# The front of a fused attention and gMLP kernel: load order, tile 0 and 1's epsilon, and the turns of tiles 1 to 3

## The chip, the cores and the metric

The kernel runs on one core of one Trainium2 chip. A time is the device time of one execution in microseconds; the time of a kernel is the median of its runs. Engines are named as in the profile: PE (TensorE, matmuls), PEld (TensorE's weight loads), DVE (VectorE), ACT (ScalarE), POOL (GpSimd), SP (SyncE, which here only issues loads and stores).

## The reference

```python
def reference(A_x, A_wqkv, A_wo, B_x, B_w_in, B_w_sp, B_b_sp, B_w_out):
    x = A_x                                   # (1, 2048, 512) bf16
    xn = layernorm(x)                         # eps 1e-5, no scale
    return x + A(xn, A_wqkv, A_wo) + B(xn, B_w_in, B_w_sp, B_b_sp, B_w_out)

def A(x, wqkv, wo):    # 32 heads of 16; each position looks at 8 positions back, 2 apart
    q, k, v = split(x @ wqkv)
    logits = q . k[pos - 2 * w] / 4           # w = 0..7, masked before the start
    return (softmax(logits) . v[pos - 2 * w]) @ wo

def B(x, w_in, w_sp, b_sp, w_out):            # w_in: 512 x 1376, so two halves of 688
    z = gelu(x @ w_in)
    z1, z2 = z[..., :688], layernorm(z[..., 688:])
    g = w_sp @ z2 + b_sp                      # mixes the 2048 positions
    return (z1 * g) @ w_out
```

## The kernel before

The 2048 tokens are 16 tiles of 128 tokens. The front of the kernel brings each tile from its load to the first matmul, in these steps (i is the tile):

- `x{i}`: the load of the tokens, 128 x 512, issued by SP (`load_x`). `wz0` and `wz1` load the z2 half of `w_in` (512 rows as four blocks of 128, "kc", two blocks in each load); they are issued by ACT. A memset on VectorE into `w_z[1]` stands ahead of them: the first load waits for it.
- `b{i}`, `ag{i}`: VectorE's statistics (`bn_stats`) and their aggregate to mean and variance (`bn_aggr`).
- `gr{i}`: GpSimd adds epsilon (L179) and raises to the power -1/2 (L180).
- `n{i}`: VectorE normalises the tile (L183); for tile 0 in two halves, `n0a` and `n0` (L187).
- `T{i}`: TensorE turns the tile in four 128x128 transposes (L216) into a bank of PSUM (`aux`, two in turn); `Tc{i}`: ACT copies it to `xnT` (L219). Tile 0 is turned in two halves, `T0a` and `T0`. From tile 8 on the turn is a transposing DMA (`t{i}`).
- `z{i}`: eight matmuls on TensorE (L234), four kc by two halves of 344 columns, into one of three PSUM buffers `mm`; `h{i}`: ACT's gelu of it (L251). For tile 0, `z0a` is the four matmuls of kc 0 and 1, and `z0b` those of kc 2 and 3.

Ahead of the first turn TensorE runs ten matmuls on constants (`wu`, L463), and after `T0` the turn of the bias (`B`, L470, whose 4 KB load `b16` GpSimd issues) and three short spins (`wd`, L463).

Every engine runs its steps strictly in the order of a list written out by hand (`pe`, `act`, `dve`, `pool`, `sp`); a step also waits for the steps it names. No scheduler moves anything. Behind the front come the z1 half, the projections to q, k and v, the attention products, the mixing with `w_sp` and the two output projections, all in the same lists; they are not touched.

Of the kernel before, what the change touches and what calls it, by code (L numbers as in the profile page):

```python
# [26 lines left out]
FH = 688  # L27
F = 2 * FH
# [4 lines left out]
EPS = 1e-5  # L33
# [9 lines left out]
def kernel(  # L43
# [48 lines left out]
    w_z = [wts[:, C * (3 * D + n * FH):C * (3 * D + (n + 1) * FH)].rearrange("p (k f) -> p k f", k=C) for n in (1, 0)]  # L92
# [17 lines left out]
    z2 = z2_r[:].rearrange("p (i f) -> p i f", i=NT)  # L110
# [4 lines left out]
    xs = z1_r[:, 0:NT * D].rearrange("p (i d) -> p i d", i=NT)  # L115
# [14 lines left out]
    mm = [ps.tile([P, 2, D], F32, name=f"mm{n}") for n in range(3)]  # L130
# [39 lines left out]
    LX = [0, 1, 2, 3, 4, 5, 6, 6] + [8] * 4 + [12] * 4  # L170

    def bn(i):
        V.bn_stats(stats[:, i, :], xs[:, i, :])  # L173

    def ag(i):
        V.bn_aggr(mv[:, i, :], stats[:, i, :])

    def root(i, n):
        G.tensor_scalar(rstd[:, i:i + n], mv[:, i:i + n, 1], EPS, 1.0, ALU.add, ALU.mult)  # L179
        G.tensor_tensor(rstd[:, i:i + n], rstd[:, i:i + n], mhalf[:, 0:n], ALU.pow)  # L180

    def norm(eng, i):
        eng.tensor_scalar(xn[i % 8], xs[:, i, :], mv[:, i, 0:1], rstd[:, i:i + 1], ALU.subtract, ALU.mult)  # L183

    def norm_half(n):
        c = slice(n * D // 2, (n + 1) * D // 2)
        V.tensor_scalar(xn[0][:, c], xs[:, 0, c], mv[:, 0, 0:1], rstd[:, 0:1], ALU.subtract, ALU.mult)  # L187

    for i in range(NT):
        op_(f"b{i}", [f"x{LX[i]}"], lambda i=i: bn(i))  # L190
        op_(f"ag{i}", [f"b{i}"], lambda i=i: ag(i))
        op_(f"gr{i}", [f"ag{i}"], lambda i=i: root(i, 1))
        if i == 0:
            op_("n0a", ["gr0"], lambda: norm_half(0))
            op_("n0", ["n0a"], lambda: norm_half(1))
        else:
            op_(f"n{i}", [f"gr{i}"] + ([tok(i - 8)] if i >= 8 else []), lambda i=i: norm(V, i))
        if i >= NPE:
            op_(f"t{i}", [f"n{i}"], lambda i=i: SP.dma_start_transpose(xnT[:, :, i * P:(i + 1) * P], xn[i % 8]))
# [21 lines left out]
    def make_T0():  # L221
        t0 = psum("aux", "T0a", "Tc0a", ["n0a"], lambda t: turn(0, t, (0, 1)))
        t1 = psum("aux", "T0", "Tc0", ["T0a", "n0"], lambda t: turn(0, t, (2, 3)))
        op_("Tc0a", ["T0a"], lambda: turned(0, t0, 0, 2))
        op_("Tc0", ["T0"], lambda: turned(0, t1, 2, 4))

    def make_T(i):
        t = psum("aux", f"T{i}", f"Tc{i}", [f"n{i}"], lambda t: turn(i, t))
        op_(f"Tc{i}", [f"T{i}"], lambda: turned(i, t))


    def z_half(t, i, part, hh, kcs=range(C)):
        for kc in kcs:
            PE.matmul(t[:, hh, 0:FHALF], xnT[:, kc, i * P:(i + 1) * P], w_z[part][:, kc, hh * FHALF:(hh + 1) * FHALF],  # L234
                      start=(kc == 0), stop=(kc == C - 1))
# [2 lines left out]
        for hh in range(2):  # L238
            z_half(t, i, part, hh)

    for n in range(2):
        op_(f"wz{n}", [], lambda n=n: A.dma_start(w_z[1][:, 2 * n:2 * n + 2, :], wi_d[:, 2 * n:2 * n + 2, FH:F]))
    op_("wk", [], lambda: SP.dma_start(w_k, wq_d[:, :, D:2 * D]))
    op_("wq", [], lambda: SP.dma_start(w_q, wq_d[:, :, 0:D]))
    op_("wv", [], lambda: SP.dma_start(w_v, wq_d[:, :, 2 * D:3 * D]))
# [9 lines left out]
    def make_z(i):  # L255
        t = psum("mm", f"z{i}", f"h{i}", [tok(i), "wz0", "wz1", "Bc"], lambda t: z_part(t, i, 1))
        op_(f"h{i}", [f"z{i}"], lambda: z2_gelu(i, t))

    def make_z0():
        t0 = psum("mm", "z0a", "h0", ["Tc0a", "wz0"], lambda t: [z_half(t, 0, 1, hh, (0, 1)) for hh in range(2)])  # L260
        op_("z0b", ["z0a", tok(0), "wz1"], lambda: [z_half(t0, 0, 1, hh, (2, 3)) for hh in range(2)])
        op_("h0", ["z0b"], lambda: z2_gelu(0, t0))

    def z2_bn(i):
        for hh in range(2):
            V.bn_stats(zst[:, i, hh, :], z2[:, i, hh * FHALF:(hh + 1) * FHALF])
        V.bn_aggr(zmv[:, i, :], zst[:, i].rearrange("p a b -> p (a b)"))
# [200 lines left out]
    def make_B():  # L468
        def turn_b(t):
            PE.transpose(t.bitcast(BF16)[:, 0:NT], b16[:], ident[0:NT, 0:NT])  # L470
# [118 lines left out]
    for n, (t, c) in enumerate(pieces):  # L589
# [1 line left out]
        op_(f"Sl{n}", [f"Fl{n}"], lambda n=n, c=c: (SP, A, SP)[n].dma_start(out2[il * P:(il + 1) * P, c], o_of(il)[:, c]))  # L591


    pe = """wu T0a T0 B wd z0a T1 z0b T2 z1 T3 z2 T4 z3 T5 z4 T6 z5 T7 z6 z7 y0 y1 z8 z9 z10 z11 z12 z13 z14
        k0 k1 q0 q1 k2 k3 q2 q3 k4 k5 q4 q5 k6 k7 q6 q7
        v0 v1 v2 v3 v4 v5 v6 v7 z15 y2 y3 y4 y5 y6 y7 y8 y9 y10 y11 y12 y13 y14 y15
        M0 M1 M2 M3 M4 M5 M6 M7 M8 M9 M10 M11 M12 M13 M14 M15
# [1 line left out]
    for n in pe:  # L599
        a, x = n[0], n[1:]  # L600
        if n in do:
            continue
        if n == "T0a":
            make_T0()
        elif a == "T":
            make_T(int(x))
        elif n == "z0a":
            make_z0()
        elif a == "z":
            make_z(int(x))  # L610
        elif a == "y":
            make_y(int(x))
        elif a in "qkv":
            make_heads(a, int(x))
        elif a == "M":
            make_M(int(x))
        elif a == "B":
            make_B()
    op_("GL", [], lambda: A.preload_act_table(ACT.Gelu_apprx_tanh))
    op_("EL", ["yg15"], lambda: A.preload_act_table_set("natural_log_exp_and_others"))  # L620

    act = """wz0 wz1 GL Tc0a Tc0 Bc Tc1 Tc2 h0 Tc3 h1 Tc4 h2 Tc5 h3 Tc6 h4 Tc7 h5 h6 h7 yg0 yg1 h8 h9 sq8 h10 h11 sq9 h12 h13 h14 sq10
        kc0 sq11 kc1 qc0 sq12 qc1 kc2 sq13 kc3 sq14 qc2 qc3 kc4 kc5 qc4 qc5 kc6 kc7 qc6 qc7
        vc0 vc1 zn8 vc2 zn9 vc3 zn10 vc4 zn11 vc5 vc6 vc7 h15 sq15
        yg2 yg3 yg4 yg5 yg6 yg7 yg8 yg9 zn12 yg10 zn13 yg11 zn14 yg12 zn15 yg13 yg14 yg15 EL
        e0 G0 i0 G1 e1 i1 G2 G3 G4 G5 G6 G7 G8 G9 G10 G11 G12 G13 G14 G15""".split()
    act += [f"E{i}" for n in (0, 1) for i in groups[n]]
    dve = """b0 ag0 b1 ag1 n0a n0 b2 ag2 n1 b3 n2 ag3 b4 ag4 n3 b5 ag5 n4 b6 ag6 b7 n5""".split()
    for i in range(6, NT):
        dve += [f"ag{i + 1}"] * (i + 1 < NT) + [f"b{i + 2}"] * (i + 2 < NT) + [f"n{i}"]  # L630
    dve += """zt0 zt1 zt2 zt3 zt4 zt5 zn0 zn1 zn2 zn3 zt6 zt7 zn4 zn5 zn6 zn7
# [62 lines left out]
```

## Time and profile before

| | |
|---|---|
| median of 3 runs | 200.33 us (200.26 to 200.45) |
| the profiled execution | 200.27 us, of which the profile's span is 198.5 us |
| PE busy | 194.2 us, 98% of the span |
| DVE busy | 178.4 us, 90% |
| ACT busy | 89.4 us, 45% |
| POOL busy | 49.3 us, 25% |
| granted TensorE clock over the span | 1.000 |

Times in the profile are counted from the start of the span. A row of the timeline has start, length, engine, line, operation and tiles, and in brackets how long the engine stood idle just before and what released it; equal operations that follow one another are merged with their count. Matmuls are pipelined: a merged row ends when its last result is out, and the next row can start before that. A load's line is that of the issue; the time to landing is from the issue to the moment its last engine reports.

### The profile page before, as it was taken

The numbers are of one execution on the slowest core, as the hardware profiler recorded it, in microseconds if no ns is written. First come the engines' busy times: TensorE is split into PE (matmuls) and PEld (weight loads), VectorE is DVE, ScalarE is ACT, GpSimd is POOL, SyncE is SP. The second block draws the span as 40 slices with busy tenths as digits, with TensorE's granted clock in tenths as the row PEclk, the third lists the DMA queues.
The fourth block names the chain that finished last, engine by engine and source line by source line (L and its number), as shares of the span: only waits on it lengthen the run. The fifth ranks groups of instructions, "written<-read, shape, count | busy, mean of one in ns | idle before, by whom it ended". The sixth has DMA issues, their size and how long they took to land.

```text
span 198.5 us, 4606 instructions
## 1 busy us (share of the span) xinstructions
PE 194.2 (98%) x1957; PEld 122.0 (61%) x1960; DVE 178.4 (90%) x205; ACT 89.4 (45%) x130; POOL 49.3 (25%) x83
## 2 busy tenths in 40 slices
PE   8999999999999999999999999999999999999993
PEld 2566666666666666666666666666666654444442
DVE  4899896999979999988999999999999999997244
ACT  2587797875559885991462311111222110044000
POOL 5567222005992249363000000010111000000000
PEclk9999999999999999999999999999999999999999
DMA  5999566860979999998299999999999969204233
GB/s 156 355 363 212 102 135 137 96 131 6 182 141 173 204 168 179 169 181 162 48 229 229 165 220 236 193 181 225 262 185 109 242 116 259 45 3 147 68 106 106
DMA packets 69076, 32.87 MB, mean 166 GB/s; under 512 B 57312, under 2 KB 67072, under 8 KB 68928
## 3 DMA queue, kind: packets, MB, share of 16 engines
q1 hardware_dynamic: 65680, 24.15, 58.2%
q0 software_dynamic: 2688, 7.70, 21.2%
q10 hardware_dynamic: 688, 0.74, 1.3%
q8 instruction: 15, 0.25, 0.5%
q14 instruction: 5, 0.04, 0.1%
HBM read 10.13 MB, written 2.10 MB: 62 GB/s over the span
## 4 chain that ended last, share of the span: by engine, by line
PE 94%; DMA 2%; DVE 1%; issue 1%; POOL 0%; SPq 0%; DVEq 0%
PE mm L479 38%; PE mm L325 21%; PE mm L234 18%; PE mm L544 7%; PE mm L533 6%; PE aux L533 2%; DMA z<-in_A_x_dram 2%; PE mm L540 1%; PE aux L216 1%; SPq L166 0%; DVE stats L173 0%; DVE z L590 0%; POOL rstd L180 0%; DVE z L183 0%; POOL rstd L179 0%
## 5 line engine op out<-in xcount | busy, mean ns | idle before, releaser
L479 PE MATMUL mm<-z,wsp 128*128 128x344 bf16 x512 | 74.8, 309 | 0.0
L479 PEld LDWEIGHTS <-wsp 128*128 128x128 bf16 x512 | 50.1, 98 | 24.6
L325 PE MATMUL mm<-xnT,wts 128*32 128x512 bf16 x768 | 41.7, 379 | 0.0
L234 PE MATMUL mm<-wts,xnT 128*128 128x344 bf16 x256 | 38.8, 309 | 0.0
L325 PEld LDWEIGHTS <-wts 128*32 128x32 bf16 x768 | 28.5, 138 | 13.0 <-issue 0.3
L430 DVE TENSOR_TENSOR prod<-vp,a_sb 128x4096 bf16<-128x4096 bf16 x16 | 36.2, 2283 | 0.0
L495 ACT ACTIVATE qk<-mm,b_col 128x688 bf16<-128x688 f32 x16 | 13.2, 830 | 42.8 <-PE mm L479 41.3
L234 PEld LDWEIGHTS <-xnT 128*128 128x128 bf16 x256 | 24.7, 98 | 11.8 <-issue 0.4
L363 DVE TENSOR_TENSOR prod<-qk 128x4096 bf16<-128x4096 bf16 x12 | 26.9, 2287 | 0.3 <-ACT qk L338 0.2
L434 DVE TENSOR_TENSOR prod<-prod,prod 128x8192 bf16<-128x8192 bf16 x6 | 26.5, 4420 | 0.1
L338 ACT CAST qk<-mm 128x1024 bf16<-128x1024 f32 x16 | 16.2, 1012 | 8.2 <-PE mm L325 8.2
L490 POOL DMA_DIRECT2D qk<-qk x8 | 3.9, 496 | 54.2 <-DMA qk<-z 49.6
L544 PE MATMUL mm<-wts,xnT 32*128 32x512 bf16 x192 | 14.5, 374 | 0.0
L314 ACT ACTIVATE z<-mm 128x688 bf16<-128x688 f32 x16 | 11.6, 744 | 3.4 <-PE mm L234 3.0
L533 PEld LDWEIGHTS <-qk 128*128 128x128 bf16 x75 | 7.2, 98 | 9.1 <-issue 0.8
L251 ACT ACTIVATE z<-mm 128x688 bf16<-128x688 f32 x16 | 11.9, 745 | 1.8 <-PE mm L234 1.8
L533 PE MATMUL mm<-wts,qk 128*128 128x512 bf16 x52 | 12.2, 379 | 0.3 <-issue 0.2
L173 DVE BATCH_NORM_STATS2 stats<-z 128x6 f32<-128x512 bf16 x16 | 10.7, 671 | 1.7 <-DMA z<-in_A_x_dram 1.7
L371 POOL DMA_DIRECT2D prod<-prod x10 | 9.4, 1132 | 8.4 <-DVE prod L363 8.4
L544 PEld LDWEIGHTS <-xnT 32*128 32x128 bf16 x256 | 6.5, 93 | 7.3
L578 ACT CAST z<-mm 128x512 bf16<-128x512 f32 x6 | 3.3, 600 | 13.7 <-PE mm L544 13.7
L338 ACT CAST vp<-mm 128x1024 bf16<-128x1024 f32 x8 | 8.1, 1011 | 2.7 <-PE mm L325 2.7
(92 smaller groups left out, 186.9 us busy)
## 6 DMA issues: line engine op xcount, KB each, us to landing
prod<-prod POOLq DMA_DIRECT2D x10, 512.0 KB, 8.5
wts<-in_A_wo_dram SPq DMA_DIRECT2D x4, 512.0 KB, 6.7
wsp<-in_A_x_dram SPq DMA_DIRECT2D x2, 1024.0 KB, 6.1
out_dram<-z SPq DMA_DIRECT2D x15, 128.0 KB, 1.8
wts<-in_A_wqkv_dram SPq DMA_DIRECT2D x3, 512.0 KB, 8.8
z<-in_A_x_dram SPq DMA_DIRECT2D x2, 512.0 KB, 6.4
wsp<-z POOLq DMA_DIRECT2D x2, 512.0 KB, 7.1
wsp<-wts POOLq DMA_DIRECT2D x2, 512.0 KB, 9.4
```

The source lines that it names most:

```text
L234: PE.matmul(t[:, hh, 0:FHALF], xnT[:, kc, i * P:(i + 1) * P], w_z[part][:, kc, hh * FHALF:(hh + 1) * FHALF], start=(kc == 0), stop=(kc == ...
L251: A.activation(z2[:, i, :].rearrange("p (a b) -> p a b", a=2), t[:, :, 0:FHALF], ACT.Gelu_apprx_tanh, **total)
L314: op_(f"yg{i}", [f"y{i}"], lambda: A.activation(z1u[:, i, 0:FH].rearrange("p (a b) -> p a b", a=2), t[:, :, 0:FHALF], ACT.Gelu_apprx_tanh))
L325: PE.matmul(t[32 * g:32 * g + 32, dd, :], w, r, start=(kc == 0), stop=(kc == C - 1), tile_position=(0, 32 * g))
L338: op_(f"{a}c{p}", [f"{a}{p}"], lambda: A.copy(home(a, p), t[:].rearrange("p d (t s) -> p d t s", t=2)))
L363: V.tensor_tensor(pr, q, k, ALU.mult)
L430: return lambda: V.tensor_tensor(dst, vp[:, :, th, off:off + GS], a_sb[:, th, W - 1 - w].unsqueeze(1).broadcast_to([P, DH, GS]), ALU.mult)
L434: return lambda: V.tensor_tensor(dst, dst, x, ALU.add)
L479: PE.matmul(t[:, hh, 0:FHALF], w[:, k, (j % 2) * P:(j % 2 + 1) * P], z2[:, k, hh * FHALF:(hh + 1) * FHALF], start=(k == 0), stop=(k == NT ...
L495: lambda: A.activation(gs[j % 3].rearrange("p (a b) -> p a b", a=2), t[:, :, 0:FHALF], ACT.Identity, bias=b_col[:, j:j + 1]))
L533: PE.matmul(po[i][:, c], uT[th][:, m, t0:t0 + P], wout[:, m, c], start=(start and m == 0), stop=(stop and m == MF - 1))
L544: PE.matmul(po[groups[n][g]], op[32 * g:32 * g + 32, th, d, s * P:(s + 1) * P], wo_r[32 * g:32 * g + 32, d, :], start=False, stop=(d == DH ...
```

## The change

- SP now issues z2's weights, in three loads instead of two: `x0 x1 x2 wz0 wz1 x3 wz2 x4 ...`. `wz0` holds kc 0 and 1, `wz1` kc 2, `wz2` kc 3. ACT issues no load at the front, and the memset that held them back is gone.
- For tiles 0 and 1 VectorE adds epsilon right behind the aggregate; GpSimd only raises to the power.
- Tile 2's statistics are taken in two halves, `b2a` and `b2`, of 256 columns (`stats2`), and the order on VectorE becomes `... n0a n0 b2a n1 b2 ag2 b3 ag3 n2 ...`, further on `ag6 n5 b7` instead of `ag6 b7 n5`.
- On TensorE, `z0b` runs kc 2 in both halves, then kc 3. Tile 1's and tile 2's matmuls are cut in two: `Z1` is the first four of tile 1 (all kc of the first half), `z1` the other four; `Z2` is the first two of tile 2 and `z2` the other six. The order becomes `z0a T1 z0b Z1 T2 z1 Z2 T3 z2 T4 z3`.

```diff
-    V.memset(w_z[1][:, 0, 0:D], 0.0)
...
+    def bn2(n):
+        V.bn_stats(stats2[:, n, :], xs[:, 2, n * D // 2:(n + 1) * D // 2])
+
     def ag(i):
-        V.bn_aggr(mv[:, i, :], stats[:, i, :])
+        V.bn_aggr(mv[:, i, :], stats2[:].rearrange("p a b -> p (a b)") if i == 2 else stats[:, i, :])
+        if i in (0, 1):
+            V.tensor_scalar(rstd[:, i:i + 1], mv[:, i, 1:2], EPS, None, ALU.add)

     def root(i, n):
-        G.tensor_scalar(rstd[:, i:i + n], mv[:, i:i + n, 1], EPS, 1.0, ALU.add, ALU.mult)
+        if i not in (0, 1):
+            G.tensor_scalar(rstd[:, i:i + n], mv[:, i:i + n, 1], EPS, 1.0, ALU.add, ALU.mult)
         G.tensor_tensor(rstd[:, i:i + n], rstd[:, i:i + n], mhalf[:, 0:n], ALU.pow)
...
-    for n in range(2):
-        op_(f"wz{n}", [], lambda n=n: A.dma_start(w_z[1][:, 2 * n:2 * n + 2, :], wi_d[:, 2 * n:2 * n + 2, FH:F]))
+    for n, (a, b) in enumerate(((0, 2), (2, 3), (3, 4))):
+        op_(f"wz{n}", [], lambda a=a, b=b: SP.dma_start(w_z[1][:, a:b, :], wi_d[:, a:b, FH:F]))
...
-        op_("z0b", ["z0a", tok(0), "wz1"], lambda: [z_half(t0, 0, 1, hh, (2, 3)) for hh in range(2)])
+        op_("z0b", ["z0a", tok(0), "wz1", "wz2"], lambda: [z_half(t0, 0, 1, hh, (kc,)) for kc in (2, 3) for hh in range(2)])
...
+    SPLIT = {1: 4, 2: 2}
+
+    def make_Z(i):
+        def some(t, a, b):
+            for n in range(a, b):
+                z_half(t, i, 1, n // C, (n % C,))
+        s = SPLIT[i]
+        t = psum("mm", f"Z{i}", f"h{i}", [tok(i), "wz0", "wz1", "Bc"], lambda t: some(t, 0, s))
+        op_(f"z{i}", [f"Z{i}"], lambda: some(t, s, 2 * C))
+        op_(f"h{i}", [f"z{i}"], lambda: z2_gelu(i, t))
...
-    pe = """wu T0a T0 B wd z0a T1 z0b T2 z1 T3 z2 T4 z3 ...
+    pe = """wu T0a T0 B wd z0a T1 z0b Z1 T2 z1 Z2 T3 z2 T4 z3 ...
-    act = """wz0 wz1 GL Tc0a Tc0 Bc Tc1 Tc2 h0 Tc3 h1 ...
+    act = """GL Tc0a Tc0 Bc Tc1 Tc2 h0 Tc3 h1 ...
-    dve = """b0 ag0 b1 ag1 n0a n0 b2 ag2 n1 b3 n2 ag3 b4 ag4 n3 b5 ag5 n4 b6 ag6 b7 n5""".split()
+    dve = """b0 ag0 b1 ag1 n0a n0 b2a n1 b2 ag2 b3 ag3 n2 b4 ag4 n3 b5 ag5 n4 b6 ag6 n5 b7""".split()
-    sp = """x0 x1 x2 x3 x4 x5 x6 x8 wy x12 ...
+    sp = """x0 x1 x2 wz0 wz1 x3 wz2 x4 x5 x6 x8 wy x12 ...
```

More of the change, by code (lines that the diff above doesn't have):

```diff
@@ L74 @@
     stats = sb.tile([P, NT, 6], F32, name="stats")
+    stats2 = sb.tile([P, 2, 6], F32, name="stats2")
     mv = sb.tile([P, NT, 2], F32, name="mv")
@@ L189 @@
     for i in range(NT):
-        op_(f"b{i}", [f"x{LX[i]}"], lambda i=i: bn(i))
+        if i == 2:
+            op_("b2a", ["x2"], lambda: bn2(0))
+            op_("b2", ["b2a"], lambda: bn2(1))
+        else:
+            op_(f"b{i}", [f"x{LX[i]}"], lambda i=i: bn(i))
         op_(f"ag{i}", [f"b{i}"], lambda i=i: ag(i))
@@ L591 @@
         op_(f"Sl{n}", [f"Fl{n}"], lambda n=n, c=c: (SP, A, SP)[n].dma_start(out2[il * P:(il + 1) * P, c], o_of(il)[:, c]))
-    pe = """wu T0a T0 B wd z0a T1 z0b T2 z1 T3 z2 T4 z3 T5 z4 T6 z5 T7 z6 z7 y0 y1 z8 z9 z10 z11 z12 z13 z14
+    pe = """wu T0a T0 B wd z0a T1 z0b Z1 T2 z1 Z2 T3 z2 T4 z3 T5 z4 T6 z5 T7 z6 z7 y0 y1 z8 z9 z10 z11 z12 z13 z14
         k0 k1 q0 q1 k2 k3 q2 q3 k4 k5 q4 q5 k6 k7 q6 q7
@@ L608 @@
             make_z0()
+        elif a == "Z":
+            make_Z(int(x))
         elif a == "z":
@@ L620 @@
     op_("EL", ["yg15"], lambda: A.preload_act_table_set("natural_log_exp_and_others"))
-    act = """wz0 wz1 GL Tc0a Tc0 Bc Tc1 Tc2 h0 Tc3 h1 Tc4 h2 Tc5 h3 Tc6 h4 Tc7 h5 h6 h7 yg0 yg1 h8 h9 sq8 h10 h11 sq9 h12 h13 h14 sq10
+    act = """GL Tc0a Tc0 Bc Tc1 Tc2 h0 Tc3 h1 Tc4 h2 Tc5 h3 Tc6 h4 Tc7 h5 h6 h7 yg0 yg1 h8 h9 sq8 h10 h11 sq9 h12 h13 h14 sq10
         kc0 sq11 kc1 qc0 sq12 qc1 kc2 sq13 kc3 sq14 qc2 qc3 kc4 kc5 qc4 qc5 kc6 kc7 qc6 qc7
@@ L637 @@
     pool = ["b16"] + [f"gr{i}" for i in range(NT)] + "zr0 zr4 kh2 f01 zr8 f10 kh3 f11 f20 f21 zr12 f30 f31 LO5 V00 V01 V02 V03".split()
-    sp = """x0 x1 x2 x3 x4 x5 x6 x8 wy x12 wk wq wv t8 t9 t10 t11 t12 t13 t14 t15 W0 kh0a kh0b W1 kh1 vh
+    sp = """x0 x1 x2 wz0 wz1 x3 wz2 x4 x5 x6 x8 wy x12 wk wq wv t8 t9 t10 t11 t12 t13 t14 t15 W0 kh0a kh0b W1 kh1 vh
         W2 W3 LO0 LO1 W4 U0 W5 LO2 LO3 U1 U2 W6 LO4 U3 U4 W7 U5 U6 U7 U8 U9 U10 R0 U11 U12 U13 V10 V11 R1 U14 V12 U15 V13""".split()
```

## The prediction

> **What bounds the kernel now.** I first read the chain that ended last: nearly all of it is TensorE, so what matters at the front is the moment from which TensorE never waits again. The page gives the shares:
>
> ```profile
> PE 94%; DMA 2%; DVE 1%; issue 1%; POOL 0%; SPq 0%; DVEq 0%
> ```
>
> The pieces of that chain in order of time (start us, us, what) show where it passes to TensorE for good:
>
> ```profile
> 1.20 0.41 SPq L166
> ...
> 1.66 3.98 DMA z<-in_A_x_dram
> ...
> 7.58 0.42 DVE z L183
> ...
> 8.05 0.40 PE aux L216 x4
> 8.45 1.17 PE mm L234 x8
> ...
> 11.06 0.22 PE aux L216 x4
> ```
>
> The load of tokens 2 (issued 1.66, landed 5.64) releases its statistics, then GpSimd's root, then its normalisation at 7.58, then its turn on TensorE at 8.05. From there only TensorE's own work is in the chain, 0.22 us for four transposes and 1.17 us for eight matmuls (0.146 each). So the change can only move this front, and everything behind moves with it one for one.
>
> The timeline of TensorE gives what it loses before the steady state (start us, us, engine, line, ...):
>
> ```profile
> 6.01 0.35 PE L463 MATMUL mm<-const-bfloat16-1.0 128*128 128x128 bf16 x3
> 6.19 0.75 PE L234 MATMUL mm<-wts,xnT 128*128 128x344 bf16 x4
> 6.92 0.40 PE L216 MATMUL aux<-ident,z 128*128 128x128 bf16 x4
> 7.20 0.74 PE L234 MATMUL mm<-wts,xnT 128*128 128x344 bf16 x4
> 8.05 0.40 PE L216 MATMUL aux<-ident,z 128*128 128x128 bf16 x4
> 8.28 1.33 PE L234 MATMUL mm<-wts,xnT 128*128 128x344 bf16 x8
> 9.49 0.40 PE L216 MATMUL aux<-ident,z 128*128 128x128 bf16 x4
> 9.73 1.33 PE L234 MATMUL mm<-wts,xnT 128*128 128x344 bf16 x8
> 10.90 0.39 PE L216 MATMUL aux<-ident,z 128*128 128x128 bf16 x4
> ```
>
> These rows are z0a, T1, z0b, T2, z1, T3, z2, T4. From z0a's start at 6.19 to T4's at 10.90 pass 4.71 us. The work in it is 24 matmuls (3.50) and three turns (0.67), together 4.17. So 0.54 us are lost: 0.15 ahead of T1, 0.04 ahead of z0b, about 0.28 ahead of T2, and crumbs. That 0.54 us is all that the change can win, unless z0a itself starts earlier.
>
> **What sets z0a.** The rows of the other engines (idle before and its releaser in brackets):
>
> ```profile
> 3.66 0.18 DVE L176 BATCH_NORM_AGGREGATE mv<-stats 128x2 f32<-128x6 f32 x1
> 3.76 0.66 DVE L173 BATCH_NORM_STATS2 stats<-z 128x6 f32<-128x512 bf16 x1
> 4.45 0.18 DVE L176 BATCH_NORM_AGGREGATE mv<-stats 128x2 f32<-128x6 f32 x1
> 4.83 0.60 DVE L187 TENSOR_SCALAR z<-z,mv,rstd 128x256 bf16<-128x256 bf16 x2 [0.19 <-POOL rstd L180]
> ...
> 6.48 0.38 DVE L183 TENSOR_SCALAR z<-z,mv,rstd 128x512 bf16<-128x512 bf16 x1
> ```
> ```profile
> 3.94 0.19 POOL L179 TENSOR_SCALAR rstd<-mv 128x1 f32<-128x1 f32 x1 [1.62 <-DVE mv L176]
> 4.21 0.58 POOL L180 TENSOR_TENSOR rstd<-rstd,mhalf 128x1 f32<-128x1 f32 x1
> ```
> ```profile
> 5.55 0.65 ACT L219 COPY xnT<-aux 128x256 bf16<-128x256 bf16 x2 [1.75 <-PE aux L216]
> 7.36 0.59 ACT L219 COPY xnT<-aux 128x512 bf16<-128x512 bf16 x1 [1.07 <-PE aux L216]
> ```
> ```profile
> L219 ACT COPY xnT<-aux x5: 373/586/586, 5.6 to 9.9; 128x512 bf16<-128x512 bf16 x3, 128x256 bf16<-128x256 bf16 x2
> ```
> ```profile
> 5.89 0.09 PEld L470 LDWEIGHTS <-b 16*128 16x128 bf16 x1 [0.30 <-DMA b<-in_B_b_sp_dram]
> ```
>
> The first copy of tile 0 (5.55, 128x256, so the shortest of its line, 0.37) is done at 5.92, but TensorE's turn of the bias (L470) waits until 5.89 for its own small load, and the three spins behind it (6.01) hand over at 6.19. Tile 0's statistics therefore have some 0.2 us to spare.
>
> **Epsilon on VectorE.** GpSimd loses its add, worth 4.21 - 3.94 = 0.27 us of the chain to the power. VectorE gains two 128x1 adds; the nearest row is
>
> ```profile
> L282 DVE TENSOR_SCALAR zmean<-zsum 128x4 f32<-128x4 f32 x2 | 0.3, 161 | 0.0
> ```
>
> so I take 0.16 us each. Each depends on the aggregate in front of it: it starts 0.18 + 0.03 behind the aggregate's start (0.03 is the gap from statistics to aggregate), and the next operation about 0.10 later, as 3.66 to 3.76. So b1 moves from 3.76 to 3.97, ag1 to 4.66, the second add stands at 4.87, and n0a cannot start before 4.97. GpSimd alone would allow 4.03 + 0.10 + 0.58 + 0.04 = 4.75. Hence the edit makes n0a 0.14 us later (4.97 against 4.83), not earlier: the second add is queued ahead of it. The ends are 0.08 earlier (adds that cost nothing) and 0.14 later; I take the later one. It pushes the copy's end from 5.92 to 6.06, and a first matmul to about 6.17, still inside the cover of bias and spins. So z0a stays at 6.19, cost nothing; were that cover gone, 0.14 us.
>
> **Loads in one queue.** How long issues took to land, first the second and third token loads (1.20, 1.66), then the next three, then the two weight parts issued by ScalarE:
>
> ```profile
> DMA to landing us min/median/max: 2.1/3.1/4.0
> DMA to landing us min/median/max: 4.8/4.8/4.9
> DMA to landing us min/median/max: 4.1/4.6/5.2
> ```
>
> Tokens 1 took 2.1 us; tokens 2 took 4.0, sharing the engines with the weights. And what was moved in 2.5 to 4.0 us, against 6.5 to 7.0 when only one queue was left with work:
>
> ```profile
> DMA packets 238, 0.25 MB, mean 170 GB/s; under 512 B 19, under 2 KB 238, under 8 KB 238
> DMA packets 201, 0.19 MB, mean 376 GB/s; under 512 B 20, under 2 KB 201, under 8 KB 201
> ```
>
> Behind two token loads on the same queue, tokens 2 should take about 2.1 us, landing near 3.8. At 376 GB/s 128 KB take 0.35 us, 344 KB 0.94, 172 KB 0.47. So wz0 lands at 4.75, wz1 5.2, tokens 3 5.6, wz2 6.0, tokens 4 6.4. If the thin stretch belongs to the first weight packets and comes again behind tokens 2, all but tokens 2 are 0.8 us later (1.5 us at 170 GB/s instead of 376 lose 1.5 x 206/376): 5.6, 6.0, 6.4, 6.8, 7.2. I take the middle. Either way wz0 is there before 6.19 and wz2 before z0b's 6.99. SyncE issues three loads more ahead of the later ones; one costs about 0.47 (1.20 to 1.66), so tokens 4 go out 1.4 us later, at 1.66 + 5 x 0.47 = 4.0, and still land before their statistics, which stand behind n2 (now 7.58) on VectorE. The removed memset on VectorE ran long before the first statistics, and ScalarE is idle there: nothing.
>
> The Trainium skill (DMA: Bandwidth & Descriptors, Bandwidth) speaks against cutting the weights: batch transfers to 1 MiB or more, since each has about 2 us of fixed cost and bytes over 436 GB/s besides. As an estimate from that page, three parts one after the other would take 2.8 + 2.4 + 2.4 = 7.6 us, put wz2 near 9.7, and make the kernel about 2.4 us slower. The trace does not bear it out for loads queued on one ring, and I keep the rows: three token loads, issued 0.47 apart, each took the same 4.8 to 4.9 to land, so they overlapped.
>
> **The new order on TensorE.** Tile 1's normalisation now waits for half of tokens 2's statistics only. The other bn_stats form is
>
> ```profile
> L266 DVE BATCH_NORM_STATS2 zst<-z 128x6 f32<-128x344 bf16 x16 | 7.1, 489 | 0.0
> ```
>
> by which a 256-wide half takes some 0.35 to 0.45 us. n0a and n0 end at about 5.5, the half follows, n1 starts at 5.85 to 5.95 and ends by 6.35 (now it runs from 6.48 to 6.86). So T1 no longer waits: it starts when z0a's four matmuls are out, 6.19 + 0.58 = 6.77. z0b follows at 6.99 and is out at 7.57.
>
> But the next piece, Z1, needs tile 1's copy. The rows say what a turn costs until its copy is done: 6.92 to 7.36 + 0.59 = 7.95, that is 1.03 us, and about 0.06 more to the first matmul. So Z1 starts at 6.77 + 1.09 = 7.86, and TensorE stands for 0.29 us. Z1's four matmuls are out at 8.44; T2 follows. Its normalisation is ready: second half at 6.2, aggregate near 6.6, GpSimd's add and power (3.94 to 4.79, some 0.9 us with the handing over), n2 from about 7.75 to 8.15. z1's four matmuls run 8.66 to 9.25, and Z2 needs tile 2's copy: 8.44 + 1.09 = 9.53, another 0.28 us standing. Z2's two are out at 9.82, T3 at 10.04, z2's six at 10.92, T4 starts at 10.92 against 10.90.
>
> So the sum is: gained 0.15 + 0.04 (T1, z0b) + 0.28 (T2) + 0.07 of crumbs; paid 0.29 + 0.28 on the two copies; z0a 0. Net 0.03 us later, with 0.04 either way on each copy wait and up to 0.14 on z0a. In plain words, the wait for tokens 2 is replaced by the wait for ScalarE's copies, which was hidden behind it. The profiled execution took 200.27 us (span 198.5), the median of the runs is 200.33 (200.26 to 200.45). Adding 0.03 gives **200.3 us**.
>
> **Rivals.**
> - *No copy wait, faster.* All 0.54 us goes and z0a comes a little earlier. For it: in the chain the load of tokens 2 is the only piece of DMA, and it lands 1.8 us earlier. Against: the 1.03 us from turn to copied tile, of which z0b covers 0.80. It decides if that delay is below 0.8. Time: 200.33 - 0.54 = 199.8.
> - *Weights late, slower.* wz0 and wz2 now stand behind tokens in SyncE's queue. If each part keeps its present time to landing (up to 5.2 us), wz2, issued near 1.66 + 4 x 0.47 = 3.55, lands at 8.75. Z1's wait covers z0b until 7.28; from there each us costs one: up to 1.47, 201.8; half of that, 201.0 to 201.1, is the likelier size. For it: the thin stretch when the weights start. Against: 376 GB/s from one queue alone.
> - *Tokens 2 do not come earlier.* If they still land at 5.64, the half statistics start then rather than at 5.5, n1 still ends before 6.77 and n2 by about 8.4, no later than T2's 8.44: again 200.3. This belongs to my forecast.
>
> **Chances.** Copy waits take the place, within 0.4 us: 0.52. Faster rival and what is like it: 0.21. Weights late, or the bias load or the adds beyond their cover: 0.27. A difference under 0.2% (0.4 us) is about what a measurement of this kernel can tell from no change. The likeliest case alone spans 200.1 to 200.6; to hold 8 in 10 I go from 199.75, the faster rival, to 201.0, the likelier size of the slower.
>
> **What would show it.** Right: tokens 2's statistics have no wait for a DMA, T1 starts near 6.8 directly behind z0a, two gaps of about 0.3 us on TensorE ahead of Z1 and Z2 with ScalarE's copy as the cause, T4 near 10.9. Wrong: T4 before 10.5 (the copies were not waited for), or z0a after 6.4 or z0b after 7.3 with a DMA as releaser (loads late), or n0a after 5.1.

## The result, and the profile after

The changed kernel takes 201.25 us (median of 12 runs, 200.69 to 202.75), the kernel before, run beside it, 200.3 us (12 runs, 199.99 to 201.2). The ratio is 1.0057, 95% interval 1.0031 to 1.0084: slower by about 0.95 us, where 200.3 was forecast. The profiled execution took 201.36 us with a span of 199.6 us, against 200.27 and 198.5 before; so it has 1.1 us to explain. One run reported further down (204.55 us, in `p3`) had a lower granted clock, 0.992 where the others there had 0.998 or more, and its ratio leaves it out.

The front first, since the forecast was made there. TensorE's timeline of the changed kernel, from the spins ahead of z0a to tile 4's turn:

```profile
5.92 0.34 PE L484 MATMUL mm<-const-bfloat16-1.0 128*128 128x128 bf16 x3
6.10 0.74 PE L243 MATMUL mm<-wts,xnT 128*128 128x344 bf16 x4
6.68 0.39 PE L225 MATMUL aux<-ident,z 128*128 128x128 bf16 x4
6.91 1.60 PE L243 MATMUL mm<-wts,xnT 128*128 128x344 bf16 x8
8.34 0.39 PE L225 MATMUL aux<-ident,z 128*128 128x128 bf16 x4
8.56 1.31 PE L243 MATMUL mm<-wts,xnT 128*128 128x344 bf16 x6
9.71 0.39 PE L225 MATMUL aux<-ident,z 128*128 128x128 bf16 x4
9.93 1.04 PE L243 MATMUL mm<-wts,xnT 128*128 128x344 bf16 x6
10.81 0.39 PE L225 MATMUL aux<-ident,z 128*128 128x128 bf16 x4
```

T4, the last row, starts at 10.81, 0.09 us earlier than before (10.90). The front has won a little, and the kernel is still 1.1 us longer. The rows that follow behind T7 on TensorE's timeline, first before, then after, show where most of it goes (the view ends at 30 us, so the last row of each is cut off there):

```profile
15.34 13.00 PE L234 MATMUL mm<-wts,xnT 128*128 128x344 bf16 x88
28.27 1.96 PE L325 MATMUL mm<-xnT,wts 128*32 128x512 bf16 x32
```
```profile
15.20 4.83 PE L243 MATMUL mm<-wts,xnT 128*128 128x344 bf16 x32
20.66 8.34 PE L243 MATMUL mm<-wts,xnT 128*128 128x344 bf16 x56 [0.63 <-DMA xnT<-z]
28.93 1.31 PE L346 MATMUL mm<-xnT,wts 128*32 128x512 bf16 x20
```

Before, the 88 matmuls behind T7 run without a break. After, the flow breaks behind 32 of them: the matmuls of tile 8 wait for their turned tile, which from tile 8 on is brought by a DMA. At the rate of before (1.17 us for eight in its chain, 0.146 each) they would have started at 15.20 + 32 x 0.146 = 19.87; they start at 20.66, 0.79 later. The front was 0.14 ahead at that point (15.20 against 15.34), so the projection to k starts 0.66 us later (28.93 against 28.27), and this 0.66 stays up to the last stage. The chain of the changed kernel now has a second piece of DMA, and it is this one:

```profile
15.21 5.40 DMA xnT<-z
20.61 0.05 issue
20.66 8.34 PE mm L243 x56
```

Ahead of it the chain runs over VectorE now, which makes tile 8's normalisation, and on the page PE's share of the chain falls from 94% to 87%:

```profile
PE 87%; DVE 6%; DMA 4%; issue 1%; POOL 0%; DVEq 0%
```

The remaining 0.44 us lie behind the last calculations. The last row of the chain, VectorE's way to the end of the program (called VectorE's last row below), in before and in after, with the span of each:

```profile
core 0 of [0], span 198.5 us
195.64 0.20 DVEq L689
```
```profile
core 0 of [0], span 199.6 us
196.31 0.20 DVEq L712
```

VectorE's last row starts 0.67 later, and the span ends 1.10 later (198.47 and 199.58 us in the trace). From the start of that row to the end pass 2.83 us before and 3.27 us after. So the loss is 0.66 at tile 8 and 0.44 at the end.

**Tile 8's turn.** Its DMA is issued at the same moment in both kernels, and takes 4.2 us before and 5.4 us after. The rows of its line, before and then after:

```profile
L199 SPq DMA_TRANSPOSE xnT<-z x1: 1287/1287/1287, 15.2 to 15.2; - x1
DMA to landing us min/median/max: 4.2/4.2/4.2
```
```profile
L208 SPq DMA_TRANSPOSE xnT<-z x1: 1284/1284/1284, 15.2 to 15.2; - x1
DMA to landing us min/median/max: 5.4/5.4/5.4
```

It stands in SyncE's queue behind the loads `wk wq wv`, and lands about 0.5 us after `wv`: 19.42 behind 18.93 before, 20.61 behind 20.08 after. Before, it is needed at 15.34 + 32 x 0.146 = 20.01, so it had some 0.6 us to spare; after, it is needed at 19.87 and comes 0.7 us late. `wv` is late because the whole queue is: tokens 8 to 11 land at 12.19 instead of 10.13. What the DMA engines moved from 7.5 to 9.5 us, before and after:

```profile
DMA packets 659, 0.67 MB, mean 337 GB/s; under 512 B 26, under 2 KB 659, under 8 KB 659
```
```profile
DMA packets 298, 0.29 MB, mean 144 GB/s; under 512 B 18, under 2 KB 298, under 8 KB 298
```

All loads of the front are already issued by then (`wq` and `wv` excepted), so there is work in the queue (six transfers issued by 7.5 us and not yet landed, seven before), and less than half as much is moved. Below this is called the thin stretch.

**The end.** At the end of the program SyncE waits, one after another and in a fixed order, for the eight semaphores that SyncE's and ScalarE's loads and stores use in turn. The trace's semaphore events show the last store on the eighth of them before; it lands at 197.57, and the end comes 0.91 us later. The changed kernel has one load more, so every later transfer moves on by one: the last store is on the first of the eight, lands at 198.23, and the end comes 1.35 us later. In the trace SyncE's wait for the first of the eight ends at 198.27 there and its wait for the eighth at 198.70, one about every 0.06 us, where before only the eighth was left to wait for. That the load count is what does it was a theory at this point; the next section tests it.

### The profile page after: what moved, and what is told of

Read it like the earlier page. It is cut to its first block, busy times and chain, and to the rows that moved or that the text cites. A ratio compares the mean times of both kernels' runs of the same rounds, so it can differ in the third digit from the quotient of the medians.

```text
span 199.6 us, 4606 instructions
## 1 busy us (share of the span) xinstructions
PE 194.3 (97%) x1957; PEld 122.2 (61%) x1960; DVE 178.5 (89%) x207; ACT 89.3 (45%) x130; POOL 49.2 (25%) x81
## 3 DMA queue, kind: packets, MB, share of 16 engines
HBM read 10.13 MB, written 2.10 MB: 61 GB/s over the span
## 4 chain that ended last, share of the span: by engine, by line
PE 87%; DVE 6%; DMA 4%; issue 1%; POOL 0%; DVEq 0%
PE mm L500 37%; PE mm L346 21%; PE mm L243 13%; PE mm L565 7%; PE mm L554 6%; DVE stats L172 3%; DMA xnT<-z 3%; PE aux L554 2%; DVE z L188 1%; DMA z<-in_A_x_dram 1%; PE mm L561 1%; DVE mv L178 1%; DVE stats L175 0%; DVE z L611 0%; POOL rstd L185 0%
## 5 line engine op out<-in xcount | busy, mean ns | idle before, releaser
L243 PE MATMUL mm<-wts,xnT 128*128 128x344 bf16 x256 | 39.3, 309 | 0.8 <-DMA xnT<-z 0.6
L172 DVE BATCH_NORM_STATS2 stats<-z 128x6 f32<-128x512 bf16 x15 | 10.1, 673 | 1.6 <-DMA z<-in_A_x_dram 1.6
L185 POOL TENSOR_TENSOR rstd<-rstd,mhalf 128x1 f32<-128x1 f32 x16 | 9.1, 571 | 3.2 <-DVE rstd L180 2.1
```

## The experiments

The theory after the comparison: (1) the new order and the epsilon edit neither win nor lose; (2) one load more in the rotation costs 0.43 us at the end; (3) all loads on one queue give the thin stretch, and with it the late turn of tile 8. The rival: the weights behind the tokens, or the new order, are late in themselves, and the rest follows from the front.

### The order without the loads, and the loads without the order

`e1` is the changed kernel with the weights back on ScalarE:

```diff
+    V.memset(w_z[1][:, 0, 0:D], 0.0)
...
-    for n, (a, b) in enumerate(((0, 2), (2, 3), (3, 4))):
-        op_(f"wz{n}", [], lambda a=a, b=b: SP.dma_start(w_z[1][:, a:b, :], wi_d[:, a:b, FH:F]))
+    for n in range(2):
+        op_(f"wz{n}", [], lambda n=n: A.dma_start(w_z[1][:, 2 * n:2 * n + 2, :], wi_d[:, 2 * n:2 * n + 2, FH:F]))
...
```

> The changed kernel, but z2's weights are loaded as before (two loads, issued by ScalarE behind the memset). If the loss lies in the loads (tile 8's turned tokens late for z8, and one load more in the rotation of the eight load semaphores, which the end of the program waits for one by one), this is 200.1 to 200.4 us: z8 without a wait, last store to end of program as before (about 0.9 us). If the loss lies in the new order on TensorE and VectorE or in epsilon on VectorE, it stays near 201.2.

Measured: 200.32 us (200.09 to 201.08), ratio 1.0005 (0.9994 to 1.0016). Its matmuls behind T7 run without a break, the rate from 7.5 to 9.5 us is 350 GB/s, and from VectorE's last row to the end pass 2.82 us. Point (1) holds: order and epsilon are worth nothing by themselves.

`e2` is the kernel before with the three loads on SyncE and nothing else of the change:

```diff
-    V.memset(w_z[1][:, 0, 0:D], 0.0)
...
-    for n in range(2):
-        op_(f"wz{n}", [], lambda n=n: A.dma_start(w_z[1][:, 2 * n:2 * n + 2, :], wi_d[:, 2 * n:2 * n + 2, FH:F]))
+    for n, (a, b) in enumerate(((0, 2), (2, 3), (3, 4))):
+        op_(f"wz{n}", [], lambda a=a, b=b: SP.dma_start(w_z[1][:, a:b, :], wi_d[:, a:b, FH:F]))
...
-    sp = """x0 x1 x2 x3 x4 x5 x6 x8 ...
+    sp = """x0 x1 x2 wz0 wz1 x3 wz2 x4 x5 x6 x8 ...
```

> The kernel before, with nothing of the change but the three weight loads on SyncE's queue around tokens 3 (and no memset). If the loads are the cause: 201.0 to 201.6, tile 8's turned tokens landing after 20.3 us, z8 waiting 0.4 us or more, and some 0.4 us more between the last store's landing and the end. If the new order is the cause: 200.2 to 200.4.

Measured: 201.44 us (200.85 to 201.61), ratio 1.0048 (1.0031 to 1.0064): the whole loss is in the loads. TensorE's timeline has the same break as the changed kernel, larger, though T7 (14.78) is 0.34 us earlier than before (15.12):

```profile
15.00 4.83 PE L232 MATMUL mm<-wts,xnT 128*128 128x344 bf16 x32
20.80 8.34 PE L232 MATMUL mm<-wts,xnT 128*128 128x344 bf16 x56 [0.96 <-DMA xnT<-z]
```

The front won 0.34 us in this profile, and tile 8's turn (landed 20.75) took it back and more (the projection to k starts at 29.07, 0.80 later than before): an earlier front only waits longer there.

### One load more, by itself

`e3` is the kernel before with ScalarE's second weight load cut in two:

```diff
-    for n in range(2):
-        op_(f"wz{n}", [], lambda n=n: A.dma_start(w_z[1][:, 2 * n:2 * n + 2, :], wi_d[:, 2 * n:2 * n + 2, FH:F]))
+    for n, (a, b) in enumerate(((0, 2), (2, 3), (3, 4))):
+        op_(f"wz{n}", [], lambda a=a, b=b: A.dma_start(w_z[1][:, a:b, :], wi_d[:, a:b, FH:F]))
...
```

> The kernel before, with the second weight load cut in two (kc 2 and kc 3), still on ScalarE's queue: one load more in all, nothing else moved. If the end of the program pays for where the last store's semaphore stands in the rotation: 200.7 (200.3 + 0.43), all of it behind the last store, z8 without a wait. If the longer end of the changed kernel was chance: 200.3.

Measured: 200.87 us (200.56 to 201.6), ratio 1.0032 (1.002 to 1.0045). The end is 3.27 us behind VectorE's last row, as in the changed kernel, though the loads are still on two queues. But the third part also came late (issued 3.28, landed 8.02) and z0b waited for it, so the projection to k starts 0.32 later as well. It doesn't separate the two cleanly; the runs `n1` and `p2` below do.

### Tile 8's turn taken out of the queue's way

`e4` is the changed kernel with `wv` issued behind the eight turns:

```diff
-    sp = """x0 x1 x2 wz0 wz1 x3 wz2 x4 x5 x6 x8 wy x12 wk wq wv t8 t9 t10 t11 t12 t13 t14 t15 W0 ...
+    sp = """x0 x1 x2 wz0 wz1 x3 wz2 x4 x5 x6 x8 wy x12 wk wq t8 t9 t10 t11 t12 t13 t14 t15 wv W0 ...
```

> The changed kernel, with the 512 KB load of w_v issued behind the eight turning transfers of tiles 8 to 15 instead of ahead of them. If z8 waits because tile 8's turn is queued behind the loads: that turn lands about 1.4 us earlier (near 19.2), z8 does not wait, and the time falls by 0.6 to 0.8 us to about 200.5; the longer end stays. If the wait has another cause (the normalisation of tile 8, the transposing path itself), it stays near 201.2.

Measured: 200.90 us (200.55 to 201.07), ratio 1.002 (1.0007 to 1.0034): the turn came out as expected, the time 0.4 us above the expected 200.5. Tile 8's turn lands at 19.03 and its matmuls don't wait, although the thin stretch is there (252 GB/s):

```profile
15.53 13.00 PE L243 MATMUL mm<-wts,xnT 128*128 128x344 bf16 x88
```

So the late turn is the queue's doing. What is left is the end (3.26 us behind VectorE's last row), and a front that is 0.33 us later in this profile than in the changed kernel's (T7 at 15.31 against 14.98).

### The load count, mended

`k2` is the changed kernel with tokens 4 and 5 in one load, so as many loads as before:

```diff
-    for i, n in ((0, 1), (1, 1), (2, 1), (3, 1), (4, 1), (5, 1), (6, 2), (8, 4), (12, 4)):
+    for i, n in ((0, 1), (1, 1), (2, 1), (3, 1), (4, 2), (6, 2), (8, 4), (12, 4)):
...
```

> The changed kernel with tokens 4 and 5 in one load, nothing else. If the rotation of the semaphores costs 0.43 us: 200.8 (201.25 - 0.43), the end behind the last store back to 0.9 us from 1.35; z8 still waits 0.5 us or more. If it costs nothing: 201.2.

Measured: 200.42 us (200.19 to 201.48), ratio 1.0004 (0.9983 to 1.0025), no longer told apart from the kernel before. The end is 2.82 us behind VectorE's last row again. That is 0.4 us below the expected 200.8, which left tile 8 a wait of 0.5 us: in this profile its turn lands at 19.98 and its matmuls don't wait. What waits there is z0b, 0.37 us for `wz2` (landed 7.71).

`k3` is `k2` with `wv` behind the turns too (the edit of `e4`), `k1` the same with the old order of TensorE and VectorE (`e2` with both mends).

> The changed kernel with both mends: one load for tokens 4 and 5, and w_v behind the turns. If the late turn (0.6 to 0.8) and the rotation (0.43) add up: 200.0 to 200.3, so no slower than before. If they overlap or something else is lost: 200.5 or more.

> The kernel before with the three weight loads on SyncE's queue as in the loads-only kernel, and two mends: tokens 4 and 5 come in one load (so the number of loads, and the last store's place among the eight semaphores, are those of before), and w_v is loaded behind the turns of tiles 8 to 15. If the two costs are what I take them for: TensorE's seventh turn stays near 14.8 (15.12 before), z8 does not wait, the end behind the last store is 0.9 us, and the time is 199.8 to 200.1. If the thin stretch in the loads costs more than the late turn: 200.4 or more.

Measured: `k3` 200.68 us (200.15 to 201.65), ratio 1.0011 (0.9995 to 1.0027); `k1` 200.72 us (200.14 to 201.37), ratio 1.0015 (1.0003 to 1.0028). Both came out at the slower of their two expected times: mending both costs won nothing over mending one. In `k3`'s profile the queue was slow earlier, and hit the weights themselves:

```profile
6.90 0.46 PE L243 MATMUL mm<-wts,xnT 128*128 128x344 bf16 x2
8.99 1.03 PE L243 MATMUL mm<-wts,xnT 128*128 128x344 bf16 x6 [1.63 <-DMA wts<-in_B_w_in_dram]
```

`wz2` was 5.36 us on its way there (3.5 in the changed kernel), and z0b stood for it. In `k1`'s profile the projection to k starts as early as before (28.28), and 1.1 us are lost between 85 and 88.5 us. The trace leads back to the mend. With `wv` behind the turns, the copies of k's edge that SyncE issues further on (`kh0a`, `kh0b`) land at 37.01 instead of 34.69, and VectorE's first product waits for them. VectorE is still 1.5 us late at 82.23 (80.72 before), where ScalarE waits for it, and TensorE then for ScalarE:

```profile
37.13 2.29 DVE L361 TENSOR_TENSOR prod<-qk 128x4096 bf16<-128x4096 bf16 x1 [2.53 <-DMA qk<-qk]
82.42 0.96 ACT L303 ACTIVATE z<-z,zbias,zrstd 128x688 bf16<-128x688 bf16 x1 [1.08 <-DVE zbias L291]
```

That product starts at 36.25 to 37.33 in the three kernels with `wv` behind the turns (`e4`, `k1`, `k3`), and at 34.81 to 35.57 in the other fourteen profiles. Only in `k1` did it reach TensorE: from k to the mixing with `w_sp` pass 60.22 us there, and 59.11 to 59.12 in all others. So this mend moves the cost on to the next user of the queue.

### One queue or two

`l1` is the kernel before with its two weight loads, uncut, on SyncE behind tokens 2; so one queue, but no load more:

```diff
-    V.memset(w_z[1][:, 0, 0:D], 0.0)
...
-    for n in range(2):
-        op_(f"wz{n}", [], lambda n=n: A.dma_start(w_z[1][:, 2 * n:2 * n + 2, :], wi_d[:, 2 * n:2 * n + 2, FH:F]))
+    for n, (a, b) in enumerate(((0, 2), (2, 4))):
+        op_(f"wz{n}", [], lambda a=a, b=b: SP.dma_start(w_z[1][:, a:b, :], wi_d[:, a:b, FH:F]))
...
+    sp = """x0 x1 x2 wz0 wz1 x3 x4 x5 x6 x8 ...
```

> The kernel before with the weights in two loads, as before, but on SyncE's queue behind tokens 2 (no third part, so no load more). If the thin stretch in the loads belongs to the single queue: under 320 GB/s between 7.5 and 9.5 us (337 in the kernel before), tile 8's turn lands after 20.0 and z8 waits; the end behind the last store is as before; 200.3 to 200.9. If it belongs to the third part or to the loads' number: rate, turn and time as before or faster, 199.9 to 200.1.

Measured: 200.49 us (200.26 to 201.94), ratio 1.0018 (1.0001 to 1.0034). From 7.5 to 9.5 us 291 GB/s are moved, tile 8's turn lands at 20.26 (19.42 before), and the end is at 2.83 us. The expected wait for that turn did not come, because the front is later too (T7 at 15.42 against 15.12).

`m1` is the changed kernel, with its load count, but tokens 3 to 7 issued by ScalarE; so two queues with the other half moved:

```diff
-        SP.dma_start(xs[:, i:i + n, :], x2[i * P:(i + n) * P, :].rearrange("(i p) d -> p i d", p=P))
+        (A if 3 <= i <= 6 else SP).dma_start(xs[:, i:i + n, :], x2[i * P:(i + n) * P, :].rearrange("(i p) d -> p i d", p=P))
...
-    act = """GL Tc0a Tc0 Bc ...
+    act = """GL x3 x4 x5 x6 Tc0a Tc0 Bc ...
...
-    sp = """x0 x1 x2 wz0 wz1 x3 wz2 x4 x5 x6 x8 ...
+    sp = """x0 x1 x2 wz0 wz1 wz2 x8 ...
```

> The changed kernel, with the loads of tokens 3 to 7 issued by ScalarE behind its table load, and z2's weights left on SyncE; so again two queues share the front, as in the kernel before, but with the other half of the loads moved. The number of loads is that of the changed kernel. Theory one (the thin stretch comes of one queue carrying all loads): from 7.5 to 9.5 us 300 GB/s or more are moved (changed kernel 144, before 337), tile 8's turn lands before 20.0 and z8 does not wait for it; what is left is the later end of 0.43 us: 200.6 to 200.8. Theory two (it comes of the weights standing on SyncE's queue, or of the cut in three): under 270 GB/s there, tile 8's turn after 20.0, 201.0 to 201.4.

Measured: 201.98 us (201.49 to 202.91), ratio 1.0095 (1.0067 to 1.0122). The rate from 7.5 to 9.5 us is 332 GB/s again, and tile 8's turn lands at 19.02, as theory one said. Its time was missed: ScalarE issues tokens 3 at 0.76 us, they share the engines with tokens 0 (landed 3.35 instead of 2.77), and `wz2` lands only at 8.36, so z0b waits for it:

```profile
8.40 1.03 PE L243 MATMUL mm<-wts,xnT 128*128 128x344 bf16 x6 [0.42 <-DMA wts<-in_B_w_in_dram]
```

T7 starts at 15.90. The stretch is a matter of the queues; a queue of tokens ahead of the weights costs more than it.

`m4` is the kernel before with a memset twice as wide, which sends ScalarE's weights out behind tokens 2:

```diff
-    V.memset(w_z[1][:, 0, 0:D], 0.0)
+    V.memset(w_z[1][:, 0:2, :], 0.0)
```

> The kernel before, with only its memset ahead of the weights widened from 688 to 1376 columns, so that ScalarE issues both weight loads about 0.45 us later, behind tokens 2 on the 16 DMA engines; two queues, as many loads as before, old order on TensorE. Theory one (early tokens 2 are worth 0.3 us at the front, as the front with the three loads and the old order showed, and the loss came only of the single queue and of the load more): tokens 2 land before 4.6 (before 5.64), T7 starts at 14.8 to 15.0 (before 15.12), tile 8's turn lands before 19.7, the end comes 0.91 us after the last store lands; 199.9 to 200.1. Rival (the weights come late: z0b waits for the second weight load, so the front gives back what it won): z0b after 7.3 and T7 at 15.1 to 15.5; 200.3 to 200.6.

Measured: 200.58 us (200.23 to 200.99), ratio 1.0012 (1.0002 to 1.0022). Tokens 2 land at 4.52, but the second weight load at 7.86, and z0b starts at 7.90: the rival.

### The end by itself, and the changed kernel again

`n1` is the kernel before with a load cut in two that lies near 100 us and is needed at 162 us; `n2` is the changed kernel with a load near 95 us, needed at 171 us, moved to GpSimd, whose transfers use none of the eight semaphores:

```diff
-        SP.dma_start(wout[:, 0:MF, :], B_w_out[0:MF * P, :].rearrange("(m p) n -> p m n", p=P))
+        for m0, m1 in ((0, 2), (2, MF)):
+            SP.dma_start(wout[:, m0:m1, :], B_w_out[m0 * P:m1 * P, :].rearrange("(m p) n -> p m n", p=P))
```
```diff
-        SP.dma_start(wo_r[32 * g:32 * g + 32], A_wo.rearrange("(h d) n -> h d n", d=DH))
+        (G if g == 3 else SP).dma_start(wo_r[32 * g:32 * g + 32], A_wo.rearrange("(h d) n -> h d n", d=DH))
...
```

> The kernel before, with the load of w_out's first five blocks, near 100 us and needed only from 162 us on, cut in two: one load more on SyncE, nothing else, and the front untouched. Theory (the semaphore of the last store moves on by one of the eight, so SyncE, which waits for them in a fixed order at the end, has seven more to go through after the last store lands): the end comes 1.34 us after the last landing instead of 0.91, and the kernel is 0.43 us slower, 200.7 to 200.8; q and k, the mixing and the last store stand where they stood. Rival (the later end of the changed kernel belongs to its late front or to its late last store, not to the number of loads): 0.91 us, 200.3.

> The changed kernel, with one of the four loads of w_o, near 95 us and needed only from 171 us on, issued by GpSimd instead of SyncE; so one load fewer takes one of the eight semaphores, as many as in the kernel before, and the front is that of the changed kernel. Theory: the end comes 0.91 us after the last landing instead of 1.35, and the kernel is 0.43 us faster than the changed kernel: 200.7 to 200.9; what is left above the kernel before, about 0.5 us, is tile 8's late turn. Rival: the end stays at 1.35, 201.2.

Measured: `n1` 200.55 us (200.48 to 201.55), ratio 1.0016 (1.0 to 1.0032); `n2` 200.41 us (200.2 to 200.9), ratio 1.0007 (0.9997 to 1.0017). The last row of `n1`'s chain:

```profile
core 0 of [0], span 198.7 us
195.44 0.20 DVEq L690
```

3.26 us from there to the end: the later end is there with the front untouched. The median rose by 0.19 only. In `n1`'s profile k starts 0.20 us earlier than in the profile of before, which makes up the difference, but why it does was not found; the interval holds 0.43 as well as nothing. `n2` won 0.84 us on the changed kernel, twice what the end explains. Since the changed kernel had been timed on another occasion, it was run again beside the same edit (`p2` is `n2` unchanged), with the loads in the old order and the end mended (`p3`, which is `e2` with `n2`'s edit):

> The changed kernel once more, without any edit, beside the next two on one chip. If the thin stretch is a matter of the execution, its strength differs here too, and the time lies 0.43 us above that of the changed kernel with one late load moved to GpSimd: 200.8 to 200.9. If the earlier 201.25 is what the kernel always takes: 201.2 to 201.3, with tile 8's turn after 20.3 and its matmuls waiting for it.

> The changed kernel with the one late load of w_o issued by GpSimd, as before, now beside the unedited changed kernel. The end comes 0.91 us after the last landing instead of 1.34: 0.43 us faster than the unedited one, if nothing else differs; 0.8 us faster, if the moved load does something beside.

> The kernel before, with z2's weights in three loads on SyncE's queue (no memset), and the one late load of w_o issued by GpSimd; old order on TensorE and VectorE. If the early tokens 2 are worth their 0.3 us and tile 8's turn is not late, 199.9 to 200.1, which would beat both kernels. If the thin stretch takes it back at tile 8's turn, 200.4 to 200.9.

Measured: `p1` 201.08 us (200.89 to 202.51), ratio 1.0034 (1.0014 to 1.0054); `p2` 200.49 us (200.24 to 200.92), ratio 1.0 (0.9991 to 1.0009); `p3` 200.9 us (200.16 to 204.55), ratio 1.0021 (1.0005 to 1.0037). On one chip the moved load is worth 0.59 us, with hardly a run in common. The chain's last row, first in `p1`, then in `p2`:

```profile
core 0 of [0], span 199.2 us
195.94 0.20 DVEq L712
```
```profile
core 0 of [0], span 198.5 us
195.65 0.20 DVEq L712
```

The ends are 3.27 and 2.82 us behind these rows: 0.44 of the 0.73 by which the two profiled spans differ. Of the other 0.29, 0.19 stand in the front already. `p1`'s z0a and T1, then `p2`'s:

```profile
6.26 0.92 PE L243 MATMUL mm<-wts,xnT 128*128 128x344 bf16 x4
7.02 0.39 PE L225 MATMUL aux<-ident,z 128*128 128x128 bf16 x4
```
```profile
6.24 0.76 PE L243 MATMUL mm<-wts,xnT 128*128 128x344 bf16 x4
6.83 0.39 PE L225 MATMUL aux<-ident,z 128*128 128x128 bf16 x4
```

z0a's four matmuls took 0.92 us in the one and 0.76 in the other; their weights had landed by 5.72, the trace names no wait inside them, and why they differ stays open. Tile 8 waits 0.09 us in `p1`, where the 88 matmuls behind T7 take 13.09 us, and not at all in `p2` (13.00; turns landed 20.24 and 19.94, T7 at 15.31 and 15.12). `p3` shows no gain of the loads in the old order: `wz2` lands at 7.70, z0b waits for it, T7 starts at 15.12, and tile 8 waits 0.30 us more (turn landed 20.27).

Over all seventeen profiles the end stands in two groups with nothing between. From VectorE's last row to the end pass 2.82 to 2.85 us in the ten kernels with as many loads in the rotation as before, and 3.26 to 3.28 us in the seven with one more, whatever queue, order or front they have. From 7.5 to 9.5 us the six kernels whose front uses two queues move 304 to 356 GB/s (before 337, `e1` 350, `e3` 304, `m1` 332, `m4` 352, `n1` 356); the eleven with one queue move 144 to 318, and all but `k3`, whose queue was slow earlier, below 300. From 2.5 to 12 us, which takes in the slow place wherever it lies, the two sets don't touch: 327 to 340 GB/s with two queues, 278 to 322 with one.

## Why the prediction was wrong, point by point

- **Epsilon on VectorE: right.** n0a follows tile 0's statistics by 2.03 us (2.79 to 4.82) instead of 1.90 (before, 4.83 against 2.93): 0.13 later, forecast 0.14, and hidden by bias and spins as said. z0a starts at 6.10 (forecast 6.19), because tokens 0 and the bias landed earlier. The rows; one 128x1 add took 0.15 us:

```profile
2.79 0.69 DVE L172 BATCH_NORM_STATS2 stats<-z 128x6 f32<-128x512 bf16 x1 [1.59 <-DMA z<-in_A_x_dram]
3.52 0.18 DVE L178 BATCH_NORM_AGGREGATE mv<-stats 128x2 f32<-128x6 f32 x1
3.74 0.15 DVE L180 TENSOR_SCALAR rstd<-mv 128x1 f32<-128x1 f32 x1
...
4.74 0.15 DVE L180 TENSOR_SCALAR rstd<-mv 128x1 f32<-128x1 f32 x1
4.82 0.60 DVE L192 TENSOR_SCALAR z<-z,mv,rstd 128x256 bf16<-128x256 bf16 x2
```

- **Landings up to tokens 4: right up to tokens 3, the last two 0.2 us later than the forecast's latest.** Tokens 2 at 3.86 (forecast 3.8), `wz0` 5.43 (4.75 to 5.6), `wz1` 5.90 (5.2 to 6.0), tokens 3 at 6.24 (5.6 to 6.4), `wz2` 7.05 (6.0 to 6.8), tokens 4 at 7.40 (6.4 to 7.2). So `wz2` was not there before z0b, as the prediction had it; z0b takes kc 2 first and needs `wz2` only at 6.91 + 2 x 0.146 = 7.20. The three weight parts, issued 0.47 apart, overlapped, so the serial estimate that the prediction set aside (`wz2` near 9.7) did not come:

```profile
L251 SPq DMA_DIRECT2D wts<-in_B_w_in_dram x3: 432/433/468, 2.1 to 3.6; - x3
DMA to landing us min/median/max: 3.3/3.3/3.5
```

- **The copies take the place of tokens 2: right.** T2, T3 and T4 start at 8.34, 9.71 and 10.81; forecast 8.44, 9.82 and 10.92, all 0.1 later, as z0a. TensorE's weight loads for Z1 and Z2 stand for the copies, as forecast:

```profile
7.74 0.41 PEld L243 LDWEIGHTS <-xnT 128*128 128x128 bf16 x4 [0.45 <-ACT xnT L228]
9.40 0.11 PEld L243 LDWEIGHTS <-xnT 128*128 128x128 bf16 x2 [0.45 <-ACT xnT L228]
```

In the chain of `p2`, which has the changed kernel's front, the copies of tiles 1 and 2 stand where the load of tokens 2 stood before, and Z1 starts 0.05 us behind the first:

```profile
7.25 0.59 ACT xnT L228
...
7.89 0.76 PE mm L243 x4
...
8.91 0.59 ACT xnT L228
```

- **The step that failed** is the sentence "So the change can only move this front, and everything behind moves with it one for one". It was read off the chain, which shows what came last and not what came almost as late. Two things behind the front move by themselves. First, SyncE's queue: the loads were costed up to tokens 4 and no further, although the same queue brings tile 8's turn, which had only some 0.6 us to spare. That cost 0.79 us in the profiled execution and 0.09 in `p1`'s. The 376 GB/s that the prediction took for one queue alone came from half a microsecond, in which ScalarE's queue still moved 10 of 201 packets; from 2.5 to 12 us the eleven profiles with one queue moved 278 to 322. Second, the load that was added: it was costed at its issue (0.47 us, hidden), and not at what it does to the end of the program, 0.44 us in every profiled execution of a kernel with one load more.
- **The slower rival** gave the right sign and 201.0 to 201.8, but not the mechanism: z0b started at 6.91, without a wait for `wz2`, in the profiled execution, and no wait for it shows in the three other profiles with this front (`p1`, `n2`, `p2`). It was not far off: `wz2` landed 0.15 us before it was needed, and in `k2`, `k3`, `m1`, `m4`, `e3` and `p3`, each with other loads at the front, z0b did wait for its last weights.
- **How the 0.95 us divide.** The end's 0.44 is the part that is always there, shown by the two groups, and `p2` and `n2` stand level with before once it is gone. The rest differs between executions: the changed kernel's runs lie from 200.69 to 202.75, the kernel before's from 199.99 to 201.2 beside it. In the profiled one the rest was tile 8's turn. What makes the runs at 202 to 202.75 longer, tile 8's turn, late weights as in `k3`'s profile or something else, is not known, since those were not profiled.

The thin stretch itself is shown to come with the single queue (`e1`, `m1` against `e2`, `l1` and the changed kernel, and 2.5 to 12 us over all profiles). The Trainium skill (DMA: Bandwidth & Descriptors, Issuing engines are not separate DMA queues) says that starting transfers from several engines saves only the time of issuing them. This case's traces do not agree: with at least six transfers issued by 7.5 us and not yet landed in every profile, 304 to 356 GB/s stand against 144 to 318 from 7.5 to 9.5 us. What holds the single queue up was not found. Single packets took up to 2.3 us in it (`k3`), and the 16 engines finished one load up to 1.8 us apart (tokens 5 in the changed kernel), and from 7.5 to 9.5 us the engines' busy share there is 0.51, less than half of the 1.08 before. It is left open.

No kernel tried is faster than the kernel before. `e1`, `k2`, `k3`, `n2` and `p2` can't be told from it.

## What to carry to other kernels

Read the slack of every later user of a queue before putting more into it: the chain shows only the wait that ends last, and here a transfer more than 10 us further on had some 0.6 us to spare; moving a load out of its way moved the wait to the next user (`k1`). Count what a change adds to a rotation of shared semaphores, since the end of a program can depend on which of them the last store falls. And when an edit's time varies more from run to run than the kernel's did, one profile names one cause, not the share of it; run the edit again beside its mend.

## What the runs showed of the hardware that was not expected

- One transfer more on the queues of SyncE and ScalarE moved the end of this program by 0.44 us, through the order of the last waits (2.82 to 2.85 us against 3.26 to 3.28 us from VectorE's last row to the end, seventeen profiles).
- The same bytes on one queue instead of two: 278 to 322 GB/s against 327 to 340 GB/s (single profiles, 2.5 to 12 us), with the slow place shifting between executions.
- The first matmuls differ between executions of the same front: z0a's four took 0.74 (changed kernel), 0.76 (`p2`) and 0.92 us (`p1`), with the same granted clock of 1.00 in the windows of all three profiles.
